# First projection of eight block pairs by seven products, with the second projection between the steps

## The chip, the cores and the metric

The kernel runs on one core of a Trainium2 chip. The metric is the time of one execution on the device in microseconds (us), as the median of several runs. The engines are called TensorE or PE (matrix products; PEld is its loading of the stationary operand), VectorE or DVE, ScalarE or ACT, GpSimd or POOL, and SyncE or SP. Each engine works through its own instructions in the order in which they stand in the program; an instruction that must wait for another engine holds up what stands behind it on its own engine. PE writes its products into PSUM, which has eight banks of 512 f32 values in each partition.

## The reference: what is computed

Causal attention with two masks (local for four heads, strided for four) over 8 batches of 576 tokens is followed by a bilinear feed-forward layer over all 4608 tokens:

```python
x = attn_out.transpose(0, 2, 1, 3).reshape(4608, 512)
a = x @ w_a              # 512 -> 1536, "first projection"
b = x @ w_b              # 512 -> 1536, "second projection"
out = (a * b) @ w_out    # 1536 -> 512
```

## The kernel before

Everything is in bf16 except for the sums, and the order of the work on all engines is written out by hand. The tokens are cut into nine tiles `t` of 512 (`NT` is 9), and the 1536 columns of the two projections into 12 blocks `f` of 128. The main loop at the end of the kernel runs over 16 slots for each tile: 12 slots for the blocks (`ffn_ab`, L624), then four slots `j` for the output product (`ffn_ys`, L755). Slot `16 * t + f` is block `f` of tile `t`. Between the slots `take` inserts the attention of the batches to come, and `do(slot, fn, ...)` lists further work that is put behind a slot. Where such work exists, GpSimd first makes a one-element copy (`pace`, L947) of what the slot produced.

One plain block takes two PSUM banks from a rotation of four (`mm_bank`, L607). `ab_mm` (L621) makes four products of 512 columns with `w_a` into the first and four with `w_b` into the second. ScalarE copies the first bank to SBUF (`a_sb`, L638), VectorE multiplies the copy by the second bank and writes block `f` of `pf` (L641). `a_sb` comes from the pool `fsb`, which has two buffers for each name, so the third `a_sb` tile reuses the memory of the first and must wait for its last reader.

The output product of tiles 2 to 8 (`FAST_Y`) is already made by the seven-product scheme (Strassen's, in Winograd's form): pairs of blocks are the two halves of one side, two groups of tokens the other. `fast_s` (L655, VectorE) makes the sums of `pf` that it needs in `ps`; `fast_w` (L174) once made the sums of `w_out`. `products` (L660) names the seven products "1" to "7" and their banks X, Y, Z; products "1", "6", "5" and "3" are accumulated one after the other into X without clearing it between, and after each of them the contents so far are copied out (`y_post`, L680). `y_plan` (L697) does this for tiles 2 to 7, `y_tail` (L721) for the last tile.

The attention of the last batch ends in the output slots of tile 6, so tiles 7 and 8 have none between their slots.

Of the kernel before, what the change touches and what calls it, by code (L numbers as in the profile page):

```python
# [7 lines left out]
F32 = mybir.dt.float32  # L8
BF16 = mybir.dt.bfloat16
I16 = mybir.dt.int16  # L10
ALU = mybir.AluOpType
# [13 lines left out]
VW = 128  # L25
WCH = (0, 2, 5, 9, 12)
FAST_Y = (2, 3, 4, 5, 6, 7, 8)


@with_exitstack  # L30
def kernel(
# [10 lines left out]
    nc = tc.nc  # L42
    B, H, S, D = q.shape
# [5 lines left out]
    KD = d_model // 128  # L49
    FD = d_ff // 128  # L50
    TTOK = 512
    NT = n_tok // TTOK
# [7 lines left out]
    fsb = ctx.enter_context(tc.tile_pool(name="ffn", bufs=2))  # L60
    pst = ctx.enter_context(tc.tile_pool(name="pst", bufs=1, space=bass.MemoryType.PSUM))
    dram = ctx.enter_context(tc.tile_pool(name="dram", bufs=2, space=bass.MemoryType.DRAM))

    psum4 = {}

    def open_psum(stack, **bufs):
        for nm, n in bufs.items():
# [8 lines left out]
    qz_pair = [(const.tile([128, 2, 2, S], BF16, name=f"qz{i}l"), const.tile([128, 2, 2, RS * GP], BF16, name=f"qz{i}s"))  # L76
               for i in range(2)]
# [3 lines left out]
    vl_buf = [const.tile([128, HL * 6, VW], BF16, name=f"vl{i}") for i in range(2)]  # L81
# [76 lines left out]
    XR = 4  # L158
    xT = const.tile([128, KD, XR * S], BF16)
    wa_sb = wp.tile([128, KD, d_ff], BF16)  # L160
    wb_sb = wp.tile([128, KD, d_ff], BF16)
    wo_sb = wp.tile([128, FD, d_model], BF16)

    FG = FD // 2
    HT = TTOK // 2
# [437 lines left out]
    pfs = {}  # L603
# [3 lines left out]
    def mm_bank(shape):  # L607
        nm = "tp" if used[0] % 4 == 3 and used[0] >= 0 else "mm"
        used[0] += 1
        return psum4[nm].tile(shape, F32, tag=nm, name="mm")  # L610

    def ab_mm(t, f, ab, kks, mid=None, first=0, last=KD - 1, ws=(0, 1)):
        n = min(TTOK, XR * S - TTOK * t % (XR * S))
        cuts = [(0, n)] + ([(n, TTOK - n)] if n < TTOK else [])
        for w, ps_ in [((wa_sb, wb_sb)[i], ab[i]) for i in ws]:
            if mid and ps_ is ab[1]:
                mid()
            for kk in kks:
                for c0, n in cuts:
                    x0 = (TTOK * t + c0) % (XR * S)  # L620
                    nc.tensor.matmul(ps_[:, c0:c0 + n], lhsT=w[:, kk, 128 * f:128 * (f + 1)], rhs=xT[:, kk, x0:x0 + n],  # L621
                                     start=(kk == first and c0 == 0), stop=(kk == last and c0 == cuts[-1][0]))

    def ffn_ab(t, f, mid, ab=None):  # L624
        if f == 0:
            pfs[t] = fsb.tile([128, FD, TTOK], BF16, tag="pf", name="pf", bufs=1)
        pf = pfs[t]
        if ab is None:
            ab = [mm_bank([128, TTOK]) for _ in range(2)]
            if f == 0:  # L630

                late = 1 if t == 1 else 3
                ab_mm(t, f, ab, [kk for kk in range(KD) if kk != late], last=-1)
                ab_mm(t, f, ab, [late], first=-1, last=late)
            else:
                ab_mm(t, f, ab, range(KD), mid)
        a_sb = fsb.tile([128, TTOK], F32, tag="a_sb", name="a_sb")
        nc.scalar.copy(a_sb, ab[0])  # L638
        if t in FAST_Y:
            halves = lambda x: x.rearrange("p (a i s) -> p a i s", i=2, s=16)  # L640
            nc.vector.tensor_mul(pf[:, f, :].rearrange("p (i a s) -> p a i s", i=2, s=16), halves(a_sb), halves(ab[1]))  # L641
        else:
            nc.vector.tensor_mul(pf[:, f, :], a_sb, ab[1])  # L643
        return pf[:1, f, :1]

    pss = {}

    def fast_s(t, n, gs):
        if t not in pss:
            pss[t] = nat.tile([128, FG * 5 * SW], BF16, tag="shared", name="ps").rearrange("p (n g m) -> p n g m", g=FG, n=5)  # L650
        s = pss[t][:, :, gs, :HT]
        x = pfs[t].rearrange("p (g e) (i m) -> p e i g m", e=2, i=2)[:, :, :, gs]
        a, b, op = ((x[:, 0, 1], x[:, 1, 1], ALU.add), (s[:, 0], x[:, 0, 0], ALU.subtract),
                    (x[:, 0, 0], x[:, 0, 1], ALU.subtract), (x[:, 1, 0], s[:, 1], ALU.subtract))[n]
        nc.vector.tensor_tensor(s[:, n], a, b, op=op)  # L655

    yst = {}
    ybank = {}
# [143 lines left out]
    with tc.manual_schedule(engines={ENG.PE, ENG.SP, ENG.Pool, ENG.DVE, ENG.Activation}):  # L802
# [30 lines left out]
        for nm in ORDER:  # L833
            if nm[0] == "*":
                spin(int(nm[1:]))
            elif nm == "C0":
                for x, cp, n in ((raw[0], nc.vector.tensor_copy, "k"), (raw[1], nc.scalar.copy, "q")):
                    t = nats[0, n, False][:, 0:2].rearrange("p h r d -> p (h r d)")
# [21 lines left out]
            elif nm[0] == "F":  # L860
                f = int(nm[1])
# [6 lines left out]
                elif nm == "F0B":  # L868
                    first[f].append(psum4["o"].tile([128, 512], F32, tag="o", name="ab"))
                ab_mm(0, f, first[f], {"A": (0, 1), "B": (0, 1), "b": (2,), "c": (3,)}[nm[2]],  # L870
                      ws={"A": (0,), "B": (1,)}.get(nm[2], (0, 1)))
# [5 lines left out]
        for t in range(NT):  # L877
            slots += [(ffn_ab, t, f) for f in range(FD)] + [(ffn_ys if t in FAST_Y else ffn_y, t, j) for j in range(4)]
        for b in range(1, B):
# [9 lines left out]
        def do(i, fn, *args):  # L889
            at.setdefault(i, []).append(lambda: fn(*args))  # L890

        soon = {}
        for t in FAST_Y[:-1]:
            soon[16 * t + 10] = [lambda t=t: fast_s(t, 2, slice(4, 6))]
            soon[16 * t + 11] = [lambda t=t, n=n: fast_s(t, n, slice(4, 6)) for n in (0, 1)]
# [5 lines left out]
        for b in range(FIRST_D, B):  # L901
            g0 = 16 * (b - 2)
            if b == FIRST_D:
                do(0, load_qk, b, False)
                do(1, load_qk, b, True)
                do(16, load_vl, b)
                for h in range(HL):
                    do(20 + h, load_vs, b, (h,))
            else:
                for h in range(HL):  # L910
                    do(g0 + h + (2 if b == FIRST_D + 1 else -2), load_qk, b, False, (h,))
                    do(g0 + h + (6 if b == FIRST_D + 1 else 2), load_qk, b, True, (h,))
                    do(g0 + h + 10, load_vs, b, (h,))
                do(g0 + (10 if b == FIRST_D + 1 else 7), load_vl, b)
            gs = {2: (14, 14, 15, 15, 16, 16, 17, 17, 18, 18), 3: (8, 9, 10, 11, 12, 13, 14, 15, 16, 17)}.get(b) or (
                3, 5, 7, 9, 12, 13, 14, 15, 16, 17)
            for (z, nm, part), g in zip(((0, "k", 0), (0, "k", 1), (0, "q", 0), (0, "q", 1), (1, "k", 0), (1, "k", 1),
                                         (1, "k", 2), (1, "q", 0), (1, "q", 1), (1, "q", 2)), gs):
                if (b, z, nm, part) != (FIRST_D, 0, "k", 1):
                    do(g0 + g, step_D, b, z, nm, part)  # L920
        for h in range(HL):
            do((7, 7, 8, 9)[h], spread_vs, 1, h, nc.vector.tensor_copy)
        do(1, zero_qz, 1, nc.vector, ((1, 1),))
# [7 lines left out]
        for g in range(FG):  # L931
            for n in (2, 0, 1, 3):
                do(16 * (NT - 1) + 2 * g + 1, fast_s, NT - 1, n, slice(g, g + 1))
        for t in FAST_Y[:-1]:
            for slot, n, z0, z1 in ((4, 0, 0, 2), (5, 2, 0, 2), (6, 1, 0, 2), (7, 3, 0, 2), (8, 2, 2, 4), (9, 0, 2, 4),
# [45 lines left out]
```

## Time and profile before

| | us |
|---|---|
| median of 3 runs | 327.48 (327.21 to 327.74) |
| the profiled execution | 327.27 |
| its span, first to last instruction | 325.6 |
| tile 7, slots of the blocks: from its first to its last product | 261.18 to 281.90 |
| tile 8, the same | 291.07 to 311.79 |

A group line of the profile gives source line, engine, operation, output<-input, shape and count, then total busy time and the mean ns of one instruction, then the engine's idle time before them and what ended it. A timeline line gives start, duration, engine, line, operation and count, and in brackets an idle time before it and its releaser. The duration of a product runs to the end that is modelled for it; the next product starts earlier, so what a product occupies of PE is read from the distance of the starts.

### The profile page before, as it was taken

The numbers are of one execution on the slowest core, as the hardware profiler recorded it, in microseconds if no ns is written. First come the engines' busy times: TensorE is split into PE (matmuls) and PEld (weight loads), VectorE is DVE, ScalarE is ACT, GpSimd is POOL, SyncE is SP. The second block draws the span as 40 slices with busy tenths as digits, with TensorE's granted clock in tenths as the row PEclk, the third lists the DMA queues.
The fourth block names the chain that finished last, engine by engine and source line by source line (L and its number), as shares of the span: only waits on it lengthen the run. The fifth ranks groups of instructions, "written<-read, shape, count | busy, mean of one in ns | idle before, by whom it ended". The sixth has DMA issues, their size and how long they took to land.

```text
span 325.6 us, 7280 instructions
## 1 busy us (share of the span) xinstructions
PE 319.7 (98%) x2632; PEld 204.6 (63%) x2632; DVE 247.9 (76%) x530; ACT 183.6 (56%) x305; POOL 150.3 (46%) x279
## 2 busy tenths in 40 slices
PE   8999999999999999999999999999999999999994
PEld 7754565455555587557999885569555944674474
DVE  6766887888778899898889888988877645726652
ACT  6764775478764576457644765476547733323341
POOL 8936739599857554854476247633001001100000
PEclk9999999999999999999999999999999999999999
DMA  9999999899999989999999999899155040004004
GB/s 157 159 204 200 204 182 186 153 176 132 143 210 137 140 86 98 120 215 135 105 98 204 156 97 113 181 193 103 30 128 125 2 129 0 3 0 131 0 0 131
DMA packets 110723, 40.43 MB, mean 124 GB/s; under 512 B 88672, under 2 KB 107744, under 8 KB 110688
## 3 DMA queue, kind: packets, MB, share of 16 engines
q0 software_dynamic: 85968, 19.48, 65.5%
q1 hardware_dynamic: 24576, 20.42, 24.9%
q8 instruction: 21, 0.34, 0.5%
q14 instruction: 14, 0.11, 0.1%
q10 hardware_dynamic: 144, 0.07, 0.1%
HBM read 39.51 MB, written 10.91 MB: 155 GB/s over the span
## 4 chain that ended last, share of the span: by engine, by line
PE 94%; DMA 2%; DVE 1%; ACT 1%; issue 1%; POOL 0%; POOLq 0%
PE mm L621 54%; PE mm L709 17%; PE mm L773 6%; PE st L387 4%; PE o L465 2%; PE o L524 2%; DMA shared<-in_q_dram 2%; PE mm L738 2%; PE end L738 1%; PE ab L621 1%; PE misc L154 1%; PE tp L549 1%; PE tp L295 1%; PE st L400 0%; PE tp L286 0%
## 5 line engine op out<-in xcount | busy, mean ns | idle before, releaser
L621 PE MATMUL mm<-xT,wa_sb 128*128 128x512 bf16 (+1 forms) x472 | 110.3, 357 | 0.0
L621 PE MATMUL mm<-xT,wb_sb 128*128 128x512 bf16 (+1 forms) x472 | 110.2, 357 | 0.0
L638 ACT COPY a_sb<-mm 128x512 f32<-128x512 f32 x106 | 62.1, 586 | 71.3 <-PE mm L621 70.6
L641 DVE TENSOR_TENSOR pf<-a_sb,mm 128x512 bf16<-128x512 f32 x84 | 57.3, 682 | 26.6 <-PE mm L621 22.5
L947 POOL CAST pace<-pf 1x1 f32<-1x1 bf16 x87 | 23.7, 273 | 109.6 <-DVE pf L641 93.1
L621 PEld LDWEIGHTS <-wb_sb 128*128 128x128 bf16 x480 | 46.5, 98 | 44.0 <-issue 0.2
L621 PEld LDWEIGHTS <-wa_sb 128*128 128x128 bf16 x480 | 43.7, 98 | 31.3
L408 ACT ACTIVATE p<-st 72x576 bf16<-72x576 f32 (+1 forms) x56 | 36.4, 650 | 14.7 <-PE st L387 14.5
L540 DVE TENSOR_TENSOR xT<-o,xr 64x288 bf16<-64x288 f32 x48 | 21.4, 446 | 15.3 <-ACT xr L534 14.9
L709 PEld LDWEIGHTS <-ps 128*128 128x128 bf16 x288 | 28.0, 98 | 3.1
L686 ACT COPY y_sb<-mm 128x512 f32<-128x512 f32 (+1 forms) x28 | 15.6, 556 | 17.8 <-PE mm L709 14.5
L709 PE MATMUL mm<-wf,ps 128*128 128x256 bf16 x216 | 25.5, 273 | 0.0
L533 ACT ACTIVATE xr<-o 64x576 f32<-64x576 f32 x28 | 18.1, 648 | 11.9 <-PE o L524 11.6
L773 PE MATMUL mm<-wo_sb,pf 128*128 128x512 bf16 x96 | 23.4, 379 | 0.0
L242 POOL DMA_DIRECT2D vs<-in_v_dram x24 | 19.6, 820 | 4.9 <-PE mm L709 2.4
L709 PEld LDWEIGHTS <-pf 128*128 128x128 bf16 x216 | 20.2, 98 | 2.6 <-issue 0.2
L534 ACT ACTIVATE xr<-xr 64x576 f32<-64x576 f32 x28 | 19.1, 683 | 0.9
L709 PE MATMUL mm<-wo_sb,pf 128*128 128x256 bf16 x144 | 18.5, 273 | 0.1
L211 POOL DMA_DIRECT2D kl<-in_k_dram x24 | 16.0, 667 | 5.5 <-issue 2.9
L211 POOL DMA_DIRECT2D ql<-in_q_dram x24 | 16.2, 674 | 5.0 <-DMA wo_sb<-in_moe_w_out_dram 3.9
L643 DVE TENSOR_TENSOR pf<-a_sb,mm 128x512 bf16<-128x512 f32 x22 | 14.9, 675 | 4.5 <-ACT a_sb L638 3.0
L655 DVE TENSOR_TENSOR ps<-pf 128x512 bf16<-128x512 bf16 (+1 forms) x48 | 17.7, 379 | 0.4
(147 smaller groups left out, 452.9 us busy)
## 6 DMA issues: line engine op xcount, KB each, us to landing
out_dram<-y_sb SPq DMA_DIRECT2D x12, 512.0 KB, 4.8
out_dram<-y_sb SPq DMA_DIRECT2D x11, 256.0 KB, 3.1
vl<-in_v_dram POOLq DMA_DIRECT2D x6, 384.0 KB, 7.7
kl<-in_k_dram POOLq DMA_DIRECT2D x24, 72.0 KB, 3.1
ql<-in_q_dram POOLq DMA_DIRECT2D x24, 72.0 KB, 3.1
vs<-in_v_dram POOLq DMA_DIRECT2D x24, 72.0 KB, 4.2
wo_sb<-in_moe_w_out_dram POOLq DMA_DIRECT2D x4, 384.0 KB, 9.9
natk<-in_k_dram POOLq DMA_DIRECT2D x20, 72.0 KB, 3.4
```

The costliest lines, as they stand in the source:

```text
L211: nc.gpsimd.dma_start(out=t[32 * h:32 * h + 32], in_=src[b, h].rearrange("(i y) d -> y i d", y=32))
L242: nc.gpsimd.dma_start(out=vs_buf[b % 2][:, h, :, 0:D], in_=v[b, HL + h].rearrange("(p r) d -> p r d", r=RS))
L408: nc.scalar.activation(p_flat(p)[:M, :2 * W].rearrange("p (i n) -> p i n", n=2 * n), st[:M].rearrange("p a (i n) -> p (a i) n", n=256)[:, ...
L533: nc.scalar.activation(r, sums, ACT.Ln)
L534: nc.scalar.activation(r, r, ACT.Exp, scale=-1.0)
L540: nc.vector.tensor_mul(dst.rearrange("d (p r) -> d p r", r=RS)[:, :, G * half:G * (half + 1)], o[:64, j, :W].rearrange("d (g p) -> d p g", ...
L621: nc.tensor.matmul(ps_[:, c0:c0 + n], lhsT=w[:, kk, 128 * f:128 * (f + 1)], rhs=xT[:, kk, x0:x0 + n], start=(kk == first and c0 == 0), sto ...
L638: nc.scalar.copy(a_sb, ab[0])
L641: nc.vector.tensor_mul(pf[:, f, :].rearrange("p (i a s) -> p a i s", i=2, s=16), halves(a_sb), halves(ab[1]))
L709: nc.tensor.matmul(bank[b][:, q], lhsT=lhs(g, q), rhs=rhs(g), start=k in "172" and q == 0 and g == 0, stop=g == FG - 1, skip_group_check=True)
L773: nc.tensor.matmul(ybank[j], lhsT=pf[:, f, 128 * j:128 * (j + 1)], rhs=wo_sb[:, f], start=(f == 0), stop=(f == FD - 1))
L947: nc.gpsimd.tensor_copy(pace, done)
```

## The change

For two tiles and four pairs of blocks in each (`FAST_A`: pairs 1 to 4 of tile 7, pairs 0 to 3 of tile 8; pair `g` is blocks `2g` and `2g + 1`) the first projection is made by seven products too. The 512 rows of `w_a` are split in halves `j`, the two blocks are the halves `e`, the 512 tokens the halves `k`; each product has two matmuls of 256 columns. The second projection of the pair stays plain: two times four matmuls of 512 columns.

A pair is one generator, `a_pair`. Its first half is run in the pair's even slot and its second half in the odd slot. X alternates between the two banks of a tile from `pst` (the attention's score tile before), Z and Y are the two banks of a tile from the pool `o`; all three are taken once for all pairs. The matmuls of the second projection stand between the steps of X: three after product "1", one after "6", three after "5", one after "4". ScalarE copies X out after "1", "6", "5" and "3", and Z after "7". VectorE adds Y to one quarter and Z to another, GpSimd adds `p7` to the fourth, and VectorE then multiplies both blocks. Each pair takes two `a_sb` tiles, `a[0]` and `a[1]`, one for each block.

The sums of `w_a` are made in four steps of two VectorE instructions behind slots 98, 100, 102 and 104 (tile 6), in memory that the attention no longer uses. The sums of `xT` are four VectorE instructions for each of the two tiles: behind slots 111 and 112 for tile 7, behind 124 to 127 for tile 8. In tile 8 one of the four `fast_s` of each of the pairs 0 to 3 moves from VectorE to GpSimd.

```diff
+POOL_S = (2,)
+FAST_A = {7: (1, 2, 3, 4), 8: (0, 1, 2, 3)}
...
         pf = pfs[t]
+        if f // 2 in FAST_A.get(t, ()):
+            if f % 2 == 0:
+                pairs[t, f // 2] = a_pair(t, f // 2)
+            return next(pairs[t, f // 2])
...
+    def wsum_make(n):
+        w, s_ = (lambda e, j: wav[:, j, :, :, e]), wsum_a
+        a, b, op = ((w(1, 0), w(1, 1), ALU.add), (s_[0], w(0, 0), ALU.subtract), (w(0, 0), w(1, 0), ALU.subtract),
+                    (w(0, 1), s_[1], ALU.subtract))[n]
+        for c in range(2):
+            nc.vector.tensor_tensor(s_[n][:, c], a[:, c], b[:, c], op=op)
...
+    def xsum_make(t, n):
+        s_ = xsum[t]
+        a, b = ((x_part(t, 0, 1), x_part(t, 0, 0)), (x_part(t, 1, 1), s_[:, 0]), (x_part(t, 1, 1), x_part(t, 0, 1)),
+                (x_part(t, 1, 0), s_[:, 1]))[n]
+        nc.vector.tensor_tensor(s_[:, n], a, b, op=ALU.subtract)
...
+    def a_pair(t, g):
+        pf = pfs[t]
+        if "X" not in pairs:
+            pairs["X"] = pst.tile([128, 2, 512], F32, tag="st", name="ax")
+            pairs["ZY"] = psum4["o"].tile([128, 2, 512], F32, tag="o", name="azy")
+        X, Z, Y = pairs["X"][:, g % 2, :HT], pairs["ZY"][:, 0, :HT], pairs["ZY"][:, 1, :HT]
+        a = [fsb.tile([128, TTOK], F32, tag="a_sb", name="a_sb") for _ in range(2)]
+        p7 = fsb.tile([128, HT], F32, tag="p7", name="p7")
+        quarter = lambda e, k: a[e][:, HT * k:HT * (k + 1)]
...
+        plan = {"1": (X, w(0, 0), x(0, 0)), "2": (Y, w(0, 1), x(1, 0)), "3": (X, ws(3), x(1, 1)), "4": (Z, w(1, 1), xs(3)),
+                "5": (X, ws(0), xs(0)), "6": (X, ws(1), xs(1)), "7": (Z, ws(2), xs(2))}
+
+        def P(k):
+            bank, lhs, rhs = plan[k]
+            for c in range(2):
+                nc.tensor.matmul(bank, lhsT=lhs(c), rhs=rhs(c), start=k in "172" and c == 0, stop=c == 1, skip_group_check=True)
...
+        def b_mm(e, kks):
...
+            for kk in kks:
+                nc.tensor.matmul(bank[e], lhsT=wb_sb[:, kk, 128 * f:128 * (f + 1)], rhs=xT[:, kk, x0:x0 + TTOK],
+                                 start=kk == 0, stop=kk == KD - 1)
+
+        def mult(e):
+            halves = lambda v_: v_.rearrange("p (a i s) -> p a i s", i=2, s=16)
+            nc.vector.tensor_mul(pf[:, 2 * g + e, :].rearrange("p (i a s) -> p a i s", i=2, s=16), halves(a[e]), halves(bank[e]))
+
+        P("1")
+        nc.scalar.copy(quarter(0, 0), X)
+        b_mm(0, (0, 1, 2))
+        P("6")
+        nc.scalar.copy(quarter(1, 0), X)
+        b_mm(0, (3,))
+        P("7")
+        nc.scalar.copy(p7, Z)
+        yield None
+        P("2")
+        nc.vector.tensor_tensor(quarter(0, 0), Y, quarter(0, 0), op=ALU.add)
+        P("5")
+        nc.scalar.copy(quarter(1, 1), X)
+        nc.gpsimd.tensor_tensor(quarter(1, 1), quarter(1, 1), p7, op=ALU.add)
+        b_mm(1, (0, 1, 2))
+        P("3")
+        nc.scalar.copy(quarter(0, 1), X)
+        P("4")
+        nc.vector.tensor_tensor(quarter(1, 0), Z, quarter(1, 0), op=ALU.add)
+        b_mm(1, (3,))
+        mult(0)
+        mult(1)
+        yield pf[:1, 2 * g + 1, :1]
...
-        nc.vector.tensor_tensor(s[:, n], a, b, op=op)
+        eng = nc.gpsimd if t == NT - 1 and n in POOL_S and gs.start in FAST_A[t] else nc.vector
+        eng.tensor_tensor(s[:, n], a, b, op=op)
...
+        for n in range(4):
+            do(16 * (NT - 3) + 2 * n + 2, wsum_make, n)
+        do(16 * (NT - 2) - 1, xsum_make, NT - 2, 0)
+        for n in (2, 1, 3):
+            do(16 * (NT - 2), xsum_make, NT - 2, n)
+        for n in range(4):
+            do(16 * (NT - 2) + 12 + n, xsum_make, NT - 1, n)
```

More of the change, by code (lines that the diff above doesn't have):

```diff
@@ L644, in ffn_ab @@
         return pf[:1, f, :1]
+    wav = wa_sb.rearrange("p (j c) (g e m) -> p j c g e m", c=2, e=2, m=128)
+    wsum_a = [flat.rearrange("p (c g m) -> p c g m", c=2, g=FG)
+              for flat in [vl_buf[0].rearrange("p a b -> p (a b)")[:, 12 * 128 * z:12 * 128 * (z + 1)] for z in range(2)]
+              + [t.rearrange("p a b c -> p (a b c)")[:, :12 * 128] for t in qz_pair[0]]]
+    xsum = {t: qz_pair[1][t - 7].rearrange("p a b c -> p (a b c)")[:, :8 * HT].rearrange("p (n c m) -> p n c m", n=4, c=2)
+            for t in FAST_A}
@@ new lines, in wsum_make, with x_part @@
+    def wsum_make(n):
[4 more added lines that the diff above has]
+            nc.vector.tensor_tensor(s_[n][:, c], a[:, c], b[:, c], op=op)
+    def x_part(t, j, k):
+        x0 = TTOK * t % (XR * S) + HT * k
+        return xT[:, 2 * j:2 * j + 2, x0:x0 + HT]
+    def xsum_make(t, n):
[3 more added lines that the diff above has]
+        nc.vector.tensor_tensor(s_[:, n], a, b, op=ALU.subtract)
@@ new lines @@
+    pairs = {}
+    def a_pair(t, g):
[7 more added lines that the diff above has]
+        quarter = lambda e, k: a[e][:, HT * k:HT * (k + 1)]
+        w = lambda e, j: (lambda c: wav[:, j, c, g, e])
+        ws = lambda n: (lambda c: wsum_a[n][:, c, g])
+        x = lambda j, k: (lambda c: x_part(t, j, k)[:, c])
+        xs = lambda n: (lambda c: xsum[t][:, n, c])
+        plan = {"1": (X, w(0, 0), x(0, 0)), "2": (Y, w(0, 1), x(1, 0)), "3": (X, ws(3), x(1, 1)), "4": (Z, w(1, 1), xs(3)),
[4 more added lines that the diff above has]
+                nc.tensor.matmul(bank, lhsT=lhs(c), rhs=rhs(c), start=k in "172" and c == 0, stop=c == 1, skip_group_check=True)
+        bank = [None, None]
+        x0 = TTOK * t % (XR * S)
+        def b_mm(e, kks):
+            if bank[e] is None:
+                bank[e] = mm_bank([128, TTOK])
+            f = 2 * g + e
+            for kk in kks:
[27 more added lines that the diff above has]
+        yield pf[:1, 2 * g + 1, :1]
```

## The prediction, written before the changed kernel was run

> **What bounds the kernel now.** I read first the page's busy shares and its chain that ended last, then the chain in order of time for the two tiles that change, then the timeline there, for durations and for the gap between one engine's end and the next one's start.
>
> ```profile
> span 325.6 us, 7280 instructions
> PE 319.7 (98%) x2632; PEld 204.6 (63%) x2632; DVE 247.9 (76%) x530; ACT 183.6 (56%) x305; POOL 150.3 (46%) x279
> PE 94%; DMA 2%; DVE 1%; ACT 1%; issue 1%; POOL 0%; POOLq 0%
> ...
> 261.34 20.72 PE mm L621 x96
> ...
> 291.23 20.72 PE mm L621 x96
> ```
>
> PE is the bound. In the block slots of tiles 7 and 8 the chain is 96 products of L621 in 20.72 us each, 215.8 ns apiece, with no wait. So each product taken away there is won, and each wait of PE put there is paid in full. How close the other engines follow is seen in tile 8 and at the start of the tail:
>
> ```profile
> 299.70 1.03 PE L621 MATMUL mm<-xT,wa_sb 128*128 128x512 bf16 x4
> 303.15 1.03 PE L621 MATMUL mm<-xT,wa_sb 128*128 128x512 bf16 x4
> ...
> 311.79 0.82 PE L738 MATMUL mm<-wo_sb,pf 128*128 128x256 bf16 x6
> 312.44 1.50 PE L738 MATMUL mm<-wf,ps 128*128 128x256 bf16 x12
> 313.78 0.82 PE L738 MATMUL end<-wo_sb,pf 128*128 128x256 bf16 x6
> 314.43 0.82 PE L738 MATMUL mm<-wf,pf 128*128 128x256 bf16 x6
> ...
> 312.69 0.37 ACT L686 COPY y_sb<-mm 128x256 f32<-128x256 f32 x1 [0.98 <-PE mm L738]
> ...
> 318.36 0.82 PE L738 MATMUL end<-wf,ps 128*128 128x256 bf16 x6
> 318.56 0.42 DVE L690 TENSOR_TENSOR y_sb<-mm,y_sb 128x256 f32<-128x256 f32 x1 [1.79 <-PE mm L738]
> 319.62 0.43 DVE L684 TENSOR_TENSOR y_sb<-y_sb 128x256 f32<-128x256 f32 x1 [0.64 <-ACT y_sb L686]
> 319.97 0.42 DVE L688 TENSOR_TENSOR y_sb<-end,y_sb 128x256 f32<-128x256 f32 x1
> ```
>
> A plain pair of blocks takes 303.15 - 299.70 = 3.45 us. Six products of 256 columns take 0.65 (311.79 to 312.44, 313.78 to 314.43), 109 ns each. A reader starts 0.20 to 0.25 us after PE has gone on to the next group (318.36 to 318.56 for DVE, 312.44 to 312.69 for ACT). A copy of 256 columns takes ACT 0.37, an addition takes DVE 0.42 and lets the next one start after 0.35 (319.62 to 319.97).
>
> The tail is also the nearest row for the new chain. Its product "6" (the second six of the twelve) goes into the bank that ACT copies out after "1", with six products, 0.65 us, between. The twelve took 313.78 - 312.44 = 1.34, not 1.31: the copy, ready at 313.06, cost 0.03. About 0.65 us of other products just cover one link.
>
> Two rows show what a wait for a buffer costs beyond the work waited for:
>
> ```profile
> 174.06 0.68 DVE L641 TENSOR_TENSOR pf<-a_sb,mm 128x512 bf16<-128x512 f32 x1
> 174.75 0.59 ACT L638 COPY a_sb<-mm 128x512 f32<-128x512 f32 x1 [0.23 <-DVE pf L641]
> ...
> 37.71 0.69 DVE L491 TENSOR_TENSOR xr<-o,rc 72x512 bf16<-72x512 f32 x1
> 38.45 0.42 PE L465 MATMUL o<-vs,p 72*128 72x65 bf16 x8 [0.21 <-DVE xr L491]
> ```
>
> At 174.74 the multiplication of an earlier block ends and at 174.75 ACT begins: it had waited for an `a_sb` buffer, 0.01 us. PE waiting for a bank goes on 0.05 us after its reader.
>
> **The gain.** A pair loses eight products of 512 columns (8 x 0.2157 = 1.726 us) and gets fourteen of 256 (14 x 0.109 = 1.526): 0.200 us less, 3.25 instead of 3.45. Eight pairs: 1.60 us. It lies wholly on the path.
>
> The page "TensorE: Matmul & The Clock Gate" of the Trainium skill (Back-to-back issue gap) speaks against the change: for streams with weight loads it gives about 81 ns for 128 columns and 131 for 512. Interpolated to 256 columns, about 98 ns by my estimate, a pair would lose 8 x 131 = 1.05 us and get 14 x 98 = 1.37, so the eight pairs would cost 2.6 us instead of saving. This trace has 215.7 and 109 ns, so its numbers decide.
>
> **The links inside a pair.** X is written by "1", "6", "5", "3", with a copy after each. The cover from "1" to "6" is three plain products, 0.647; from "6" to "5" one plain product, "7" and "2", 0.216 + 2 x 0.218 = 0.652; from "5" to "3" again 0.647. Needed are 0.20 to 0.25 + 0.37 + about 0.05 = 0.62 to 0.67. Each link costs 0 to 0.03; two per pair (the first is treated next) make 0 to 0.5 us, and I take 0.2.
>
> **The link from pair to pair.** This is the step that decides. `a[0]` of pair g+1 is the buffer of `a[0]` of pair g, because each pair takes two of the two. So ACT's copy after "1" of pair g+1 waits for the first multiplication of pair g, and "6" on PE waits for this copy, with all that stands behind it. On DVE that multiplication stands behind the addition of Z, which needs product "4", next to last on PE in the pair. Counted from when PE leaves "4":
> - the addition of Z starts at 0.22 (0.20 to 0.27), the multiplication 0.35 later at 0.57; its own input, the copy after "3", is there by 0.35;
> - it takes 0.687 (the mean of L641 in these tiles) and ends at 1.26;
> - ACT starts 0.01 later, copies for 0.37, and PE goes on 0.05 after that: 1.69.
> PE meanwhile has one plain product, "1" and three plain products, 0.216 + 0.218 + 0.647 = 1.08 us of work. It stands for 0.61 us (0.59 to 0.70 by the ends of these rows), three times what a pair saves. Pairs follow pairs directly three times in tile 7 and three times in tile 8: 6 x 0.61 = 3.66 us.
>
> In the rest of the stretched pair (3.25 + 0.61 = 3.86 us) nothing else is late. The copy after "6" needs the second multiplication: it starts 0.61 after the first (one of L641 at 171.77 let the next instruction go at 172.38), ends at 1.87, and "6" is read from 2.12 on. Behind the last pair of a tile stands a plain block, whose ACT copy comes four products after the pair, at 0.216 + 0.863 + 0.20 = 1.28, against 1.26: no wait. Before the first pair of tile 7 stands a plain block, long done. Before that of tile 8 stands the last copy of the output product, 0.59 us on ACT from 291.27 to 291.86: the copy after "1" ends at 292.23 and "6", due at 291.07 + 0.865 = 291.94, starts at 292.28. That is 0.34 more, once.
>
> **The other additions.** ACT gets five copies of 0.37 for two of 0.59, 0.69 us more per pair, and is idle for half of these tiles. DVE gets per pair two additions, 0.70, beside two multiplications (1.21) and two to four `fast_s` (at most 0.84): 2.75 of 3.86 us, so it is no bound. The sums of `w_a` are eight instructions of 768 elements, as L174's (0.54 to 0.56): 4.4 us in tile 6. In slots 98 to 105 the timeline has DVE idle 0.2 to 0.66 us before most multiplications; two instructions more in each second slot delay a multiplication by up to 0.7 us, and its bank is wanted two slots later, about 0.95 us after its usual end. So I set them at nothing; without that cover, 0 to 0.3 in all. The eight sums of `xT` (0.42 each) lie in output slots with DVE idle or ahead of product "6", which needs them at 265.5, about 0.6 after they end: nothing. A `fast_s` off DVE in tile 8 gains nothing, since DVE is not awaited.
>
> GpSimd's additions of two operands have no row. Its shortest row near this size is 0.28 (a selection of 128x96), its longest computation 1.83 (a MEMSET of 72x2048). The quarter for the second multiplication is copied 1.68 us before it is multiplied. At 0.28 it is hidden. At 1.83 the additions and `fast_s` of tile 8 queue up, and the three transitions there cost about 0.5 each, 1.5 us. I take hidden, since 256 elements are nearer to the short row. The page "GPSIMD Engine Reference" (Engine selection) advises VectorE for elementwise work and calls GpSimd about half as fast on two inputs; by its 4497 ns for 2048 elements I estimate 0.56 us, hidden too, and nothing here shows it yet. POOL's `pace` before these waits for the pair's multiplications, as now.
>
> **The sum:** -1.60 + 3.66 + 0.34 + 0.2 = +2.6 us. The profiled execution took 327.27 (span 325.6 and 1.67 around it), 0.21 below the median; it becomes 329.9, and the median 327.48 + 2.6 = 330.1.
>
> **Rivals.**
> 1. *More is late than this chain.* Z and Y share one tile. If "2" must wait for ACT's copy of Z although it goes to the other bank, each pair stands for 0.62 more, and the tile reaches +7.5 us. Or GpSimd is as slow as its longest row: +4.1. For it speaks that neither has a row here; against it that `xT` is written and read all the time by different engines with PE at 98%. 331.6 to 335.
> 2. *Faster: the buffer's wait is covered.* The place is "6" of the second to fourth pair of each run. If DVE released `a[0]` at or before the time at which PE gets there, only the gain and the other small terms remain: -1.60 + 0.34 + 0.2 = -1.1, 326.4. It decides when a transition costs less than (1.60 - 0.54) / 6 = 0.18 us, so the chain would have to be 0.43 shorter than 1.69. Only the addition of Z ahead of the multiplication (0.35) is near that size, and it stands in the program there. For it: two buffers did not hold ACT up for more than 0.23 us anywhere now. Against it: there the buffer's reader ran 0.9 us earlier in the cycle.
> 3. *No difference:* a transition at about 0.2. No row gives that.
>
> **How the numbers follow.** I give the chain as worked out 0.67, rival 1 0.18, rival 2 0.10, rival 3 0.05. Its own range: all terms low, -1.60 + 3.54 + 0.34 = +2.3, and with the first reader's gap smaller still some +1.8; all high, -1.60 + 4.2 + 0.4 + 0.5 + 0.3 = +3.8: 329.3 to 331.3. For 8 in 10 I go from 328.7 up to 332.6, into rival 1 as far as GpSimd's price with the other terms high; that leaves out rivals 2 and 3 and rival 1's upper end. A change of less than 0.2% (0.65 us) can't be told from none in this kernel: faster 0.10, same 0.05, slower 0.85.
>
> **What would show it.** Right: in tiles 7 and 8 PE idle about 0.6 us six times, released by ACT's copy, which itself was released by DVE's multiplication; pairs some 3.9 us apart but the last of each run 3.25 to the plain block; products of 256 columns 109 ns apart. Wrong: no idle at "6"; idle at "2" (rival 1); PE idle in tile 6 (the sums of `w_a`); the additions on POOL over 1.6 us.

## The result

The changed kernel takes 335.47 us (median of 5 runs, 334.99 to 336.58) beside 327.48 for the kernel before: a ratio of 1.0248, 95% interval 1.0227 to 1.0270. (Ratios here and below are estimated, with their intervals, from the single runs and can differ a little from the quotient of two medians.) It is slower, as forecast, but by 8.0 us instead of 2.6, and outside the range of 328.7 to 332.6. The profiled execution has a span of 333.1 us beside 325.6, so 7.5 us longer.

The page's first lines and the waits of PE, by who ended them (total us, times, longest), for the changed kernel:

```profile
span 333.1 us, 7423 instructions
PE 320.2 (96%) x2651; PEld 209.0 (63%) x2680; DVE 260.6 (78%) x558; ACT 188.9 (57%) x329; POOL 161.8 (49%) x290
...
PE azy L698 <- ACT p L722: 3.7, 8, 0.5
PE ax L698 <- ACT a_sb L716: 1.8, 6, 0.3
```

PE's busy time did not fall and its share went from 98% to 96%. Two kinds of wait are new, and both are for ACT. L698 is a product of the seven; `azy` is the tile of Z and Y, `ax` that of X, L722 the copy of Z, L716 the copy after product "1". The idle times are measured to the modelled ends of the products; by the distance of the starts a wait costs about 0.16 more. There is a third wait, before product "1"; it is over when the modelled end of the product before it is reached (268.33 + 0.38 = 268.71 below), and so is not on the list.

One whole pair of tile 7 in the timeline (pair 2, from its product "1" to that of pair 3):

```profile
268.33 0.38 PE L708 MATMUL mm<-xT,wb_sb 128*128 128x512 bf16 x1
268.72 0.38 PE L698 MATMUL ax<-xT,wa_sb 128*128 128x256 bf16 x2
268.94 0.81 PE L708 MATMUL mm<-xT,wb_sb 128*128 128x512 bf16 x3
270.06 0.38 PE L698 MATMUL ax<-qz1l,vl 128*128 128x256 bf16 x2 [0.32 <-ACT a_sb L716]
270.28 0.38 PE L708 MATMUL mm<-xT,wb_sb 128*128 128x512 bf16 x1
270.49 0.38 PE L698 MATMUL azy<-qz1l,qz0l 128*128 128x256 bf16 x2
271.33 0.38 PE L698 MATMUL azy<-xT,wa_sb 128*128 128x256 bf16 x2 [0.46 <-ACT p L722]
271.55 0.38 PE L698 MATMUL ax<-qz1l,vl 128*128 128x256 bf16 x2
...
273.26 0.38 PE L698 MATMUL ax<-xT,wa_sb 128*128 128x256 bf16 x2
```

A pair lasts 273.26 - 268.72 = 4.54 us, not 3.86. Against 3.25 us of work PE loses three times:
- before "1": due when the plain product is through at 268.33 + 0.22 = 268.55, it starts at 268.72: 0.17 to 0.19;
- before "6": due at 268.94 + 0.65 = 269.59, it starts at 270.06: 0.47;
- before "2": due at 270.49 + 0.22 = 270.71, it starts at 271.33: 0.62. Nothing here was charged for it.

ACT and DVE in the same stretch:

```profile
268.30 0.37 ACT L731 COPY a_sb<-ax 128x256 f32<-128x256 f32 x1 [0.49 <-PE ax L698]
268.53 0.42 DVE L733 TENSOR_TENSOR a_sb<-azy,a_sb 128x256 f32<-128x256 f32 x1 [0.47 <-PE azy L698]
268.87 1.28 DVE L713 TENSOR_TENSOR pf<-a_sb,mm 128x512 bf16<-128x512 f32 x2
269.64 0.37 ACT L716 COPY a_sb<-ax 128x256 f32<-128x256 f32 x1 [0.97 <-DVE pf L713]
270.48 0.37 ACT L719 COPY a_sb<-ax 128x256 f32<-128x256 f32 x1 [0.47 <-PE ax L698]
270.91 0.37 ACT L722 COPY p<-azy 128x256 f32<-128x256 f32 x1
```

The forecast chain is there step by step: addition of Z (268.53), multiplication (268.87), ACT released by it (269.64), "6" (270.06). The wait at "2" is another: the copy of Z ends at 271.28 and "2", which writes Y in the other bank of the same tile, starts at 271.33. "1" starts in the same way just behind the copy after "3" (268.30 to 268.67, "1" at 268.72), though that copy reads the other bank of X's tile; here the profile names no releaser, and it is the times that say so.

Tile 7 stretches from 20.72 to 24.36 us (261.20 to 285.56), tile 8 from 20.72 to 24.59 (294.73 to 319.32). By the sums, -1.60 for the products, 8 x 0.62 at "2", 6 x (0.47 + 0.18) from pair to pair and 0.25 in the first pair of tile 8 ("6" at 295.85 instead of 295.60) make +7.5 us, the whole growth of the span.

### The profile page after: what moved, and what is told of

It is laid out like the page before. It is cut to its first block, busy times and chain, and to the rows that moved or that the text cites. A ratio compares the mean times of both kernels' runs of the same rounds, so it can differ in the third digit from the quotient of the medians.

```text
span 333.1 us, 7423 instructions
## 1 busy us (share of the span) xinstructions
PE 320.2 (96%) x2651; PEld 209.0 (63%) x2680; DVE 260.6 (78%) x558; ACT 188.9 (57%) x329; POOL 161.8 (49%) x290
## 4 chain that ended last, share of the span: by engine, by line
PE 89%; DVE 3%; ACT 3%; issue 2%; DMA 1%; SPq 0%; ACTq 0%; DVEq 0%
PE mm L623 45%; PE mm L803 17%; PE mm L867 6%; PE st L389 4%; PE o L467 2%; PE o L526 2%; PE mm L708 2%; PE azy L698 2%; PE ax L698 2%; PE mm L832 2%; DVE pf L713 1%; DMA raw<-in_q_dram 1%; PE end L832 1%; PE ab L623 1%; PE misc L156 1%
## 5 line engine op out<-in xcount | busy, mean ns | idle before, releaser
L623 PE MATMUL mm<-xT,wb_sb 128*128 128x512 bf16 (+1 forms) x404 | 93.3, 354 | 0.5
L623 PE MATMUL mm<-xT,wa_sb 128*128 128x512 bf16 (+1 forms) x391 | 92.0, 353 | 0.7
L644 ACT COPY a_sb<-mm 128x512 f32<-128x512 f32 x90 | 52.7, 586 | 53.4 <-PE mm L623 51.4
L1048 POOL CAST pace<-pf 1x1 f32<-1x1 bf16 x83 | 26.1, 314 | 76.9 <-DVE pf L647 48.7
L623 PEld LDWEIGHTS <-wb_sb 128*128 128x128 bf16 x416 | 40.2, 98 | 36.6 <-issue 0.2
L647 DVE TENSOR_TENSOR pf<-a_sb,mm 128x512 bf16<-128x512 f32 x68 | 46.2, 680 | 8.5 <-PE mm L623 7.4
L623 PEld LDWEIGHTS <-wa_sb 128*128 128x128 bf16 x416 | 37.4, 98 | 23.8
L1048 POOL COPY pace<-y_sb 1x1 f32<-1x1 f32 x23 | 5.2, 226 | 33.2 <-DVE y_sb L778 19.8
L708 PE MATMUL mm<-xT,wb_sb 128*128 128x512 bf16 x60 | 18.5, 379 | 0.2
```

Source lines behind the costliest of these rows:

```text
L708: nc.tensor.matmul(bank[e], lhsT=wb_sb[:, kk, 128 * f:128 * (f + 1)], rhs=xT[:, kk, x0:x0 + TTOK], start=kk == 0, stop=kk == KD - 1)
L1048: nc.gpsimd.tensor_copy(pace, done)
```

## The experiments

The theory after the result: a product that writes one bank of a two-bank PSUM tile waits for every reader of the tile, and this is the missing term; the wait for the `a` buffers is a second, separate cost. The rival: ACT, with five copies a pair, is simply late, and a wait taken away at one product comes back at the next.

**Y in a tile of its own.**

```diff
-        X, Z, Y = pairs["X"][:, g % 2, :HT], pairs["ZY"][:, 0, :HT], pairs["ZY"][:, 1, :HT]
+        X, Z, Y = pairs["X"][:, g % 2, :HT], pairs["ZY"][:, 0, :HT], mm_bank([128, HT])
```

> Y is taken from the rotation of four banks, a tile of its own, instead of the second bank of Z's tile; nothing else changes. Theory (the wait is kept by tile): product "2" no longer waits for ACT's copy of Z, which held PE for 0.63 us in each of the eight pairs (0.46 idle by the modelled end); product "5" then has 0.65 us of cover for the copy after "6" and waits at most 0.03. 335.5 - 8 x 0.63 = 330.4 us. Rival (ACT's copies are late as a chain, whoever asks for them): the wait moves to product "5" and the time stays at 335.

Measured: 330.48 us beside 327.20 (the kernel before, in this and the next three runs), ratio 1.0105 (1.0088 to 1.0123). The wait at "2" is gone and did not come back at "5". PE's waits for ACT, and a part of pair 2 of tile 7:

```profile
PE ax L698 <- ACT a_sb L716: 2.2, 6, 0.4
```

```profile
270.17 0.38 PE L698 MATMUL azy<-qz1l,qz0l 128*128 128x256 bf16 x2
270.39 0.38 PE L698 MATMUL mm<-xT,wa_sb 128*128 128x256 bf16 x2
270.59 0.37 ACT L722 COPY p<-azy 128x256 f32<-128x256 f32 x1
270.61 0.38 PE L698 MATMUL ax<-qz1l,vl 128*128 128x256 bf16 x2
```

"2" (270.39) now runs ahead of the copy of Z (270.59), and "5" (270.61) starts into X's tile while that copy still runs (to 270.96): a copy out of one tile does not hold up a product into another. What was left is the case that had been predicted, and it cost somewhat more: the interval is 2.9 to 4.0 us over the kernel before, predicted were 2.6. In its profile the neighbouring pairs stand 3.97 us apart instead of 3.86 ("6" starts 1.80 after PE leaves "4", instead of 1.69), which makes 0.7 over the six. The rival, with 335, falls.

**Four `a` buffers.** Odd pairs use two key buffers of batch 6, whose last reader is long done.

```diff
-        a = [fsb.tile([128, TTOK], F32, tag="a_sb", name="a_sb") for _ in range(2)]
+        if g % 2:
+            a = [b_.rearrange("p a b -> p (a b)")[:, :2 * TTOK].bitcast(F32) for b_ in kT_buf[0]]
+        else:
+            a = [fsb.tile([128, TTOK], F32, tag="a_sb", name="a_sb") for _ in range(2)]
```

> Odd pairs take their a[0] and a[1] from two buffers that the attention no longer uses, so a buffer comes back only after two pairs; Z and Y stay in one tile. Theory: product "6" of a pair behind a pair no longer waits for VectorE's first multiplication of the pair before it, 0.47 us, six times; the waits at "2" (0.63 x 8) and at "1" (0.17 x 6) stay: 335.5 - 2.8 = 332.7 us. Rival (ACT late as a chain): 335.

Measured: 333.25 us, ratio 1.0187 (1.0161 to 1.0213). The expected 332.7 is a ratio of 1.0168 to the 327.2 of these runs, inside the interval. The profile has the eight waits at "2" and none at "6":

```profile
PE azy L701 <- ACT p L725: 3.8, 8, 0.5
```

**Both together.**

> Both: Y in a tile of its own and four a buffers. Theory: the two costs add up, 335.5 - 5.0 - 2.8 = 327.7 us; left are product "1" behind a pair (0.17 us, six times, the two banks of X being one tile) and the first pair of tile 8 (0.25). Rival: one of the two waits hides behind the other, or all move to the next link: 329 or more.

Measured: 327.96 us, ratio 1.0027 (1.0015 to 1.0040), so 0.5 to 1.3 us over the kernel before. The two costs are separate: with both causes taken away, both waits are gone from the list. Of the losses that were known, "1" behind a pair and the first pair of tile 8 are left; a third was not expected, a wait of 0.6 us in tile 8 for a bank that VectorE was late to read, of which more below:

```profile
PE mm L711 <- DVE a_sb L728: 0.6, 1, 0.6
```

**Pairs that are not neighbours.** The change as it is, with `FAST_A = {7: (1, 3), 8: (1, 3)}`.

> Only four pairs take the seven products, pairs 1 and 3 of both tiles, so that none stands right behind another; the code of a pair is as in the change. Theory: the waits at "1" and "6", which come from the pair before, are gone, the wait at "2", which is inside the pair, stays: 4 x (0.63 - 0.20) = +1.7 us over the kernel before, 329.2. Rival (ACT's copies pile up from pair to pair): a pair alone does not wait, 4 x -0.20, 326.7.

Measured: 329.35 us, ratio 1.0061 (1.0041 to 1.0081). The waits are those inside a pair only:

```profile
PE azy L698 <- ACT p L722: 1.8, 4, 0.5
```

A pair alone still loses 0.62 at "2", three times what its products save, although ACT is not late: in pair 3 of tile 7 its copy of Z starts at 274.64, 0.20 after PE has gone on from "7" (274.22 + 0.22), and "2" starts at 275.07.

**X in two tiles.** X alternates between the first banks of two tiles; Z, Y and the two banks of the second projection share the rotation of four.

```diff
-        X, Z, Y = pairs["X"][:, g % 2, :HT], pairs["ZY"][:, 0, :HT], mm_bank([128, HT])
+        X = pairs["X"][g % 2][:, 0, :HT]      # pairs["X"]: the st tile and the o tile
+        banks = [mm_bank([128, TTOK]) for _ in range(4)]
+        roles = ((1, 2, 0), (0, 1, 2), (2, 0, 1))[FAST_A[t].index(g) % 3]
+        Z, Y = banks[roles[1]][:, :HT], banks[roles[2]][:, :HT]
...
-        bank = [None, None]
+        bank = [banks[roles[0]], banks[3]]
```

> On top of the four a buffers and Y apart, X alternates between two tiles (the first bank of each of the two attention tiles) and Z and Y both come from the rotation of four banks, each taking over a bank that the pair before has done with. Theory (waits are kept by tile): product "1" behind a pair no longer waits for ACT's copy after "3" of the pair before, 0.19 us, six times: 327.96 - 1.15 = 326.8 us. It may lose up to 0.8 of that in tile 8, where VectorE runs behind. Rival (the wait at "1" has another cause, such as PE's change between products of 512 and 256 columns): 328.0.

Measured: 327.96 us beside 327.72, ratio 1.0007 (0.9995 to 1.0019), no measurable difference from the kernel before. In tile 7 a pair is now free of waits (19.93 us for the tile, 261.12 to 281.05; 20.54 with X in one tile). In tile 8 new waits for VectorE took back 0.4 of these 0.6 (21.87 us; 21.49 with X in one tile), as had been allowed for:

```profile
PE mm L623 <- DVE kT0l L730: 0.5, 1, 0.5
PE mm L713 <- DVE a_sb L730: 0.3, 1, 0.3
PE mm L713 <- DVE kT0l L730: 0.3, 1, 0.3
```

**All `fast_s` back on VectorE.** On top of X in two tiles, `POOL_S = ()`.

> As the kernel with X in two tiles, but all fast_s of tile 8 on VectorE again. In the runs so far a fast_s on VectorE took 0.78 to 1.46 us while GpSimd added two SBUF operands, 0.29 otherwise. Theory (the two engines hold each other up): VectorE gains about 0.5 us per pair and gives back 0.25, so it keeps up in tile 8; the wait of 0.6 us that PE had there goes: 326.0 us. Rival (the slow fast_s costs PE nothing): no change against the kernel with X in two tiles, or 0.2 slower.

Measured: 326.81 us, ratio 0.9969 (0.9956 to 0.9982), 0.4% below the kernel just above: taking work off VectorE had slowed VectorE. The three waits of tile 8 are gone from the list. The expected 326.0 was not reached: tile 8 (20.45 us) still loses 0.25 before "6" of its first pair and 0.27 behind its last pair. The changed kernel's tile 8, first VectorE, then GpSimd:

```profile
300.49 0.29 DVE L749 TENSOR_TENSOR ps<-pf 128x256 bf16<-128x256 bf16 x1
300.81 0.78 DVE L749 TENSOR_TENSOR ps<-ps,pf 128x256 bf16<-128x256 bf16 x1
301.62 0.29 DVE L749 TENSOR_TENSOR ps<-pf,ps 128x256 bf16<-128x256 bf16 x1
...
300.78 0.66 POOL L749 TENSOR_TENSOR ps<-pf 128x256 bf16<-128x256 bf16 x1
```

and the same work with all four on VectorE:

```profile
296.32 0.48 DVE L754 TENSOR_TENSOR ps<-pf 128x256 bf16<-128x256 bf16 x2
296.84 0.29 DVE L754 TENSOR_TENSOR ps<-ps,pf 128x256 bf16<-128x256 bf16 x1
297.17 0.29 DVE L754 TENSOR_TENSOR ps<-pf,ps 128x256 bf16<-128x256 bf16 x1
```

Three sums on VectorE and one on GpSimd took VectorE from 300.49 to 301.91, 1.42 us; four on VectorE took it 1.14, from 296.32 to 297.46.

**First multiplication first.** On top of that, `mult(0)` ahead of the addition of Z.

> As the one before, with the first multiplication ahead of the addition of Z on VectorE. It frees a bank 0.2 us earlier and Z's bank 0.6 later. Theory: nothing waits for either any more: no change, 326.0 us. Rival: the bank of the first multiplication is still awaited at the end of each run of pairs: 0.4 us faster.

Measured: 328.63 us, ratio 1.0032 (1.0014 to 1.0050): 0.6% slower, which neither expected. The first multiplication then waits for the copy after "3" with the addition of Z and the second multiplication behind it, so the second is later, and its bank is the one that the second projection of the next pair takes. In tile 7 that showed as 0.1 to 0.2 us per pair between "5" and the plain products (due at 277.24 here; they start 0.05 after the second multiplication ends, at 277.36), in tile 8 as 21.76 us instead of 20.45:

```profile
276.67 0.69 DVE L718 TENSOR_TENSOR pf<-kT0s,mm 128x512 bf16<-128x512 f32 x1
277.02 0.38 PE L703 MATMUL ax<-qz1l,vl 128*128 128x256 bf16 x2
277.41 0.81 PE L713 MATMUL mm<-xT,wb_sb 128*128 128x512 bf16 x3
```

**The same with pairs 1 to 4 of tile 8.**

> As the one before, with pairs 1 to 4 of tile 8 instead of 0 to 3, so that the first pair no longer stands behind ACT's last copy of tile 7's output (product "6" there was 0.25 us late). Theory: 0.25 us faster, 325.8 us, if VectorE has caught up by the tail; if not, the tail starts later and it is no faster.

Measured: 328.56 us, ratio 1.0029 (1.0014 to 1.0045), no gain against the kernel just above. Tile 8 lasts 21.67 us there and 21.76 in that one. "6" of the first pair is no longer late, but the waits of 0.1 to 0.5 us between and behind the pairs are there as before, and now the tail is late too: due at 313.19 + 0.86 = 314.05, it starts at 314.21.

**The best of these:** multiplications in the order of the change, pairs 1 to 4 in both tiles.

> X in two tiles, Y and Z in the rotation, four a buffers, all fast_s on VectorE, the multiplications in the order of the change, and pairs 1 to 4 of tile 8 instead of 0 to 3. Theory: product "6" of the first pair of tile 8 no longer stands behind ACT's last copy of tile 7's output, 0.25 us less than with pairs 0 to 3: ratio 0.996, 326.3 us beside a kernel before of 327.6. The step that lost time with the first multiplication put first was VectorE's second multiplication, which came later and held up the second projection of the next pair; that is taken back here. Rival: in tile 8 the later last pair leaves VectorE too late for the tail: no gain against pairs 0 to 3, 326.8.

Measured: 326.17 us beside 327.57, ratio 0.9955 (0.9941 to 0.9969), faster than both kernels. Its profile has no wait of PE in the two tiles for ACT or DVE on the list, and pair after pair stands at 3.25 us ("1" to "1"):

```profile
264.29 0.38 PE L703 MATMUL ay<-xT,wa_sb 128*128 128x256 bf16 x2
...
267.54 0.38 PE L703 MATMUL ax<-xT,wa_sb 128*128 128x256 bf16 x2
...
270.80 0.38 PE L703 MATMUL ay<-xT,wa_sb 128*128 128x256 bf16 x2
```

Tile 7 takes 19.93 us (260.83 to 280.76) and tile 8 20.20 (289.93 to 310.13), 1.31 us less in all than before. The missing 0.3 of the 1.60 lies in tile 8, behind its last pair: the second four products of the plain block there are due at 306.40 + 0.86 = 307.26 and start at 307.53, 0.05 after the first of the pair's two multiplications has ended (306.80, and its usual 0.68).

**The sums alone.** Every pair plain, all sums made and not used.

```diff
-        if f // 2 in FAST_A.get(t, ()):
+        if False:
```

> All sums of w_a and xT are made as in the change, but every pair goes the plain way and all fast_s stay on VectorE, so the sums are made and not used. Theory: VectorE has room for them in tile 6 and in the output slots: no change, 327.5 us. Rival: they delay VectorE's multiplications in tile 6 until PE waits for a bank: up to 0.5 us slower.

Measured: 327.90 us beside 327.57, ratio 1.0012 (0.9997 to 1.0027), no difference that can be told. In its profile tile 7 begins at 261.19, before 261.18.

## Why the prediction was right and wrong

- *Which way:* right, and for the reason given first. The deciding step, the link from pair to pair, held: from the time PE leaves "4" (268.11 + 0.22 = 268.33) to the start of "6" (270.06) the result has 1.73 us, predicted 1.69 (1.80 with Y apart). Of the 0.65 that this costs, 0.18 is already spent before "1"; the split was not foreseen, the sum was.
- *The step that failed* is the statement that in the rest of the stretched pair "nothing else is late". It charged nothing for "2", taking it that Y, in another bank than Z, need not wait for the copy of Z; the cost was 0.62 us in each of the eight pairs, 5.0 us in all. Rival 1 named this wait, its place and its price per pair (0.62) and its total (+7.5 us; the span grew by 7.5), but the range stopped short of it. (Its upper end was meant as the high sum, 331.3, with GpSimd's 1.5 on top, which is 332.8 and not 332.6; the measured time lies beyond either.) The argument that set its chance low was that `xT` is read and written at once by several engines. That speaks for waits in `xT`, an SBUF tile, being kept by region. It says nothing of a PSUM tile that is written in one bank while the other is read. The kernel before has no row for that: by its text its two-bank tiles are read only after their last product. With "2" free and all else as in the change, the time was 330.5, predicted 330.1; the rest is the link from pair to pair, 0.72 there instead of 0.61.
- *The gain:* right. A pair without waits lasts 3.25 us, as worked out, instead of 3.45.
- *The links inside a pair:* 0.2 us had been taken for them. They cost nothing: in the best version pairs stand at 3.25 us.
- *The first pair of tile 8:* 0.34 forecast, 0.25 measured.
- *The sums of `w_a` and `xT`:* set at nothing; right as far as the run that makes only the sums can tell (ratio 1.0012, 0.9997 to 1.0027).
- *GpSimd:* its addition of 256 f32 took 0.73 us and one of bf16 0.66, within the bounds taken (0.28 to 1.83) and hidden, as forecast. What was not seen is its effect on VectorE. In the changed kernel no cost is seen: a pair between two others lasts 4.52 us in tile 8, where GpSimd makes such sums, and 4.52 to 4.54 in tile 7, where it makes none. With the longer waits gone it cost 0.4%. The page "GPSIMD Engine Reference" of the Trainium skill (Engine selection) advises VectorE for elementwise work: 0.66 against 0.29 us on VectorE agrees with it.

Open: whether the wait goes with the tile as such or with the neighbouring bank isn't separated, since every version that lost it used another tile. Nor was the link from "3" to "1" taken away without the other moves of banks.

## What to carry to other kernels

Before a chain is counted as covered, list for each write into PSUM every reader of the whole tile it lies in, not of its bank alone; a partial sum that is filled while another is read had better have a tile of its own, as here Y (5.0 us). A chain that runs across iterations (the last reader of a buffer, a copy, the next write) is to be compared with the work between, and a scheme that saves 0.2 us per step can't afford one uncovered link of 0.6. Before work is moved from VectorE to GpSimd, see whether the two would then add SBUF operands at the same time: here four sums took VectorE 1.14 us alone, and three took it 1.42 beside GpSimd.

## What the runs showed of the hardware

GpSimd's additions held up VectorE's. In the kernel with Y apart and four `a` buffers a VectorE sum of 256 bf16 values, 0.29 us otherwise, took 1.46, from just after the start of one GpSimd addition to just after the end of a second:

```profile
300.57 1.46 DVE L752 TENSOR_TENSOR ps<-ps,pf 128x256 bf16<-128x256 bf16 x1
...
300.53 0.66 POOL L752 TENSOR_TENSOR ps<-pf 128x256 bf16<-128x256 bf16 x1
301.16 0.72 POOL L731 TENSOR_TENSOR a_sb<-a_sb,p 128x256 f32<-128x256 f32 x1
```

The two GpSimd additions end at 301.88, the VectorE sum at 302.03. VectorE's additions with an operand in PSUM were not slowed: with all `fast_s` on VectorE one took 0.42 us (from 297.38) while GpSimd added from 297.34 to 298.06:

```profile
297.34 0.72 POOL L733 TENSOR_TENSOR kT0s<-kT0s,p 128x256 f32<-128x256 f32 x1 [0.69 <-ACT kT0s L732]
297.38 0.42 DVE L730 TENSOR_TENSOR kT0l<-mm,kT0l 128x256 f32<-128x256 f32 x1
```

These additions are in f32 and the held sums in bf16, so the runs don't separate where the operands lie from their type. The page "GPSIMD Engine Reference" (Architecture) states that GpSimd's SBUF ports are shared with VectorE; the held sums are in line with that, and how the sharing is decided is not shown here.
